# A sink-and-window attention ahead of two dense layers: attention stepped by whole blocks instead of half blocks, two head pairs to a score tile

## The chip, the cores and the metric

The kernel runs on one core of one Trainium2 chip. The metric is the device time of one execution in microseconds (us). PE is the matrix engine, DVE the vector engine, ACT the scalar engine, POOL the general engine; SP issues the loads and stores. PSUM is the memory that PE writes its results to: eight banks, each of 128 partitions by 512 floats.

## What is computed

An attention with sinks and a window (batch 2, 8 heads, 768 positions, 64 features; every query sees the first 4 keys and the last 128), then a layer whose activation is a rational function, then a layer with a squared ReLU:

```python
scores = scale * np.matmul(q, k.transpose(0, 1, 3, 2))
keep = is_sink | ((rel >= 0) & (rel < 128))            # is_sink: key < 4
scores = np.where(keep, scores, -1e9)
a = np.exp(scores - np.max(scores, axis=-1, keepdims=True))
a = a / (np.sum(a, axis=-1, keepdims=True) + 1e-09)
x = np.matmul(a, v)                                    # -> 1536 tokens x 512
h = x @ w_in                                           # 512 -> 2048
P = a0 + a1*h + a2*h*h + a3*h*h*h
Q = 1.0 + abs(b0)*abs(h) + abs(b1)*h*h
x = (P / (Q + 1e-6)) @ w_out                           # 2048 -> 512
h = np.maximum(x @ w_in2, 0.0)
out = (h * h) @ w_out2
```

## The kernel before, in words

**Blocks and half blocks.** The queries are cut into 12 blocks u of 128 (six for each batch). A block has four head pairs; a pair's two heads lie in partitions 0 to 63 and 64 to 127 of the keys and queries. The first block of a batch (u = 0 and 6) sees only its own keys; every other one sees the block before it too, and the sinks. The loop `for m in range(NM): step(m)` goes by half blocks: 24 steps m of two pairs, n = 2m and n + 1. Steps 24 and 25 finish the last block and run inside the first two slots of the layers that follow (`mid` of `slot`).

**What a step issues.** `scores(n)` puts a pair's scores into one of two tiles `ss` of PSUM (two banks each, one for each head) by four matmuls on 64x64 quarters of the array; DVE then folds the window's two triangles together (one copy_predicated, L368) and takes each head's masked row maximum (two reduces, L375). `expo(n)` lets ACT take the exponentials (L392, with row sums). `trans(m - 1)` transposes the half block before through the 128x128 array (L420); ACT copies the result to SBUF and POOL cuts it into two triangles `ph`. `pv(m - 2)` multiplies `ph` by the values (L453), into PSUM tile O. `sums(u)` adds eps to a block's row sums on ACT and takes reciprocals on DVE (L409); `sinks_t(u)` transposes the sink weights and reciprocals (L413); `sinks_and_sums(u)` adds the sinks' share to O (L465) and spreads the reciprocals to all rows of w (L469), with halves of the array, 64 rows by 128 columns; ACT copies w to `rb` (L471). `result(u)` is one DVE multiply of O by `rb` (L475), which ends the block and frees O. `parts_of(u)` splits it into two parts `xh` and `xl` for the layers (a cast on ACT, L482, a subtraction on POOL, L483).

**PSUM.** The score tiles take four banks, T (transposes, w, fill) two, U one, and O one: the sums of only one block can be open at a time.

**Ahead of and behind it.** Weights are loaded and split beside the attention (`w_step`: DVE L240, L246, L252; `w_fin`: ACT L273, POOL L274). At the start, PE runs matmuls of zeros on `wz` (`fill`, L496) while data come in, and masks are made on DVE, POOL and ACT (L102 to L147). In the layers, slot k issues `act_b(k - 1)` (ACT L637, L638, then DVE L641, L643, L645), `g1(k + 1)` (L591), `act_a(k)` (ACT L607 to L611), for slots 0 and 1 `cubic` (DVE L620) and a step of the attention, then `g2(k - 2)` (L670). What is issued to an engine runs on it in that order, and waits for what it needs.

Of the kernel before, what the change touches and what calls it, by code (L numbers as in the profile page):

```python
# [12 lines left out]
ALU = mybir.AluOpType  # L13
# [5 lines left out]
TWO32 = 4294967296.0  # L19
WS = 3  # L20
NW0 = 14
DENSE = {0: 5, 2: 4}
QP = 1.0 + 1e-6

LEAST = 2.0 ** -15 * 1.125
# [12 lines left out]
def kernel(  # L38
# [254 lines left out]
    def attention(ap, extra):  # L293
# [48 lines left out]
                keys[:, :, :, P:], keys[:, :, u % NB, 0:SK].unsqueeze(2).to_broadcast([P, NPR, NB, SK])  # L342
            )

        def scores(n):
            u, pr = divmod(n, NPR)
            i = u % NB
            t = ss[n % 2]
            d = [t[:, e] for e in range(2)]
            if i == 0:  # L350
                mask, co, bw = m_0, 0, P
                for e in range(2):
                    s = slice(D * e, D * e + D)
                    nc.tensor.matmul(
                        d[e][:, 0:P], lhsT=ld[u, "q"][s, pr, :], rhs=keys[s, pr, 0, 0:P], start=True, stop=True
                    )
            else:
                mask, co, bw = (m_1 if i == 1 else m_2), P, BS
                hf = P // 2
                for g in range(2):  # L360
                    for e in range(2):
                        s, r = slice(D * e, D * e + D), slice(hf * g, hf * g + BS + hf)
                        nc.tensor.matmul(  # L363
                            d[e][hf * g:hf * g + hf, r], lhsT=ld[u, "q"][s, pr, hf * g:hf * g + hf],
                            rhs=keys[s, pr, i - 1:i + 1, :].rearrange("p i n -> p (i n)")[:, r],
                            start=True, stop=True,
                        )
                nc.vector.copy_predicated(  # L368
                    out=t[:, :, BS:BS + P], mask=tri.unsqueeze(1).to_broadcast([P, 2, P]), data=t[:, :, 0:P]
                )  # L370
            ns = []
            for e in range(2):
                ix = u * H + 2 * pr + e
                t = ap.tile([P, 160], F32, name="ns", bufs=6)
                nc.vector.tensor_tensor_reduce(  # L375
                    out=t[:, 0:bw], in0=d[e][:, co:co + bw], in1=mask, scale=-scale, scalar=3.0e38,
                    op0=ALU.add, op1=ALU.min, accum_out=nmax[:, ix:ix + 1],
                )
                ns.append(t)
            kps[n] = ns  # L380

        def expo(n):
            u, pr = divmod(n, NPR)
            w = BS if u % NB else P
            if pr == 0:
# [19 lines left out]

        def sums(u):
            rs = rs_t.pop(u)
            nc.scalar.activation(out=rs, in_=rs, func=ACTF.Identity, bias=eps)
            nc.vector.reciprocal(out=sr[u % 2][:, HS:HS + H], in_=rs)  # L409

        def sinks_t(u):
            sd = ps_t(tail=u == NU - 1)
            nc.tensor.transpose(sd[:, 0:P], sr[u % 2], ident)  # L413
            sT[u] = ap.tile([P, P], F32, name="st", bufs=2)
            nc.scalar.copy(out=sT[u], in_=sd[:, 0:P])

        def trans(m):
            d = ps_t(tail=m == NM - 1)
# [4 lines left out]
            dv = d.rearrange("p (j t) -> p j t", j=4)  # L423
            h = [
                mp.tile([P, CT], F32R, tag=tag, name="ph", bufs=2).bitcast(F32).rearrange("p (j t) -> p j t", j=4)
                if m // 2 % NB or j else None for j, tag in enumerate(("gh", "gl"))
            ]
            if h[0] is None:
                nc.scalar.copy(out=h[1], in_=dv)
            else:  # L430
                c = ap.tile([P, 4, P], F32, name="pc", bufs=2)
                nc.scalar.copy(out=c, in_=dv)
                nc.gpsimd.affine_select(
                    out=h[0], in_=c, pattern=[[0, 4], [-1, P]], base=-1, channel_multiplier=1,
                    compare_op=ALU.is_ge, fill=0.0,
                )
                nc.gpsimd.affine_select(
                    out=h[1], in_=c, pattern=[[0, 4], [1, P]], base=0, channel_multiplier=-1,
                    compare_op=ALU.is_ge, fill=0.0,
                )  # L440
            pT[m] = h
# [16 lines left out]
                            )  # L458

        def sinks_and_sums(u):  # L460
            st, w = sT.pop(u), ps_t(tail=u == NU - 1)
            for r in range(NPR):
                cs = slice(r * P, (r + 1) * P)
                if u % NB:
                    nc.tensor.matmul(  # L465
                        ops[u][:, cs], lhsT=vs[u // NB][0:HS, cs], rhs=st[0:HS], start=False, stop=False,
                        skip_group_check=True,
                    )
                nc.tensor.matmul(w[:, cs], lhsT=heads[HS:, cs], rhs=st[HS:], start=True, stop=True)  # L469
# [41 lines left out]
        bd, moe, rest, heads = None, None, None, None  # L511
        sr = [ap.tile([P, P], F32, name=f"sr{j}") for j in range(2)]

        def step(m):
            w_fin()
            nonlocal bd, moe, rest, heads
            n, (u, a) = 2 * m, divmod(m, 2)
            if m < NM:
                scores(n)
            if a == 0 and u >= 1:  # L520
                sinks(u - 1)
                sums(u - 1)
            if m < NM:
                scores(n + 1)
                if n in DENSE:
                    fill(ps_t("T"), DENSE[n])
            if m == 0:
                rest = setup_rest(*next(masks), m_1, m_2, tri)
                next(rest)
                sink_keys(0)  # L530
            if a == 0 and 2 <= u <= NU:
                parts_of(u - 2)
            if m < NM:
                expo(n)
            if m in (1, 2):
                next(rest, None)
            if 0 < m <= NM:
                trans(m - 1)
            if m == 1:
# [5 lines left out]
            if a == 0 and u + 2 < NU:  # L545
                load(u + 2)
            if a == 0 and m < NM and u % NB == 0:
                load_sinks(u // NB)
            if m >= 5:
                next(moe, None)  # L550
                next(moe, None)
            if a == 1 and u >= 1:
                sinks_and_sums(u - 1)
            if 1 < m:
                pv(m - 2)
            if m < NM:
                expo(n + 1)
            if a == 0 and u >= 1:
                sinks_t(u - 1)
            if m == NM - 1:  # L560
                g1(0)
            if m < NM and a == 1 and u % NB == 0:
                if u:
                    sink_keys(u)
                sink_values(u // NB, bd)
            extra(m)
            if a == 1 and u >= 1:
                result(u - 1)

        for m in range(NM):  # L570
            step(m)
        for j in range(2):
            slot(j, lambda: step(NM + j))
        slot(2, after=lambda: parts_of(NU - 1))


# [447 lines left out]
    with tc.tile_pool(name="ap", bufs=1) as ap:  # L1024
        NM = NU * NPR // 2

        def extra(m):
            if m == 1:
                for _ in range(NWR):
                    w_load()  # L1030
            if m % 2:
                w_until(min(WS * NA, m - 1))
            if m == NM:
                conv["on"] = False
            if m == NM + 1:
                conv["tag"], conv["on"] = "O", True

        attention(ap, extra)
# [49 lines left out]
```

## Time and profile before

| | us |
|---|---|
| median of three runs (lowest, highest) | 617.02 (616.91, 618.19) |
| the profiled execution's own time | 617.14 |
| its span on the core | 615.4 |
| stretch from the first scores of block 0 to those of block 4 | 24.01 |
| stretch from there to the first matmul of the layers | 50.00 |
| stretch from there to the first matmul of `g2(0)` | 15.12 |

The profile is of one execution. Times of rows count from the span's start; the 1.74 us between span and time lie around the program. A row's busy time can overlap the next row's on the same engine, since instructions are pipelined: the distance between two starts is what an instruction costs its engine. PE is busy nearly all the time, so a shorter path on another engine is worth something only where PE waits for it, and less work on PE is worth something where nothing else becomes late.

### The profile page before, as it was taken

Reading aid. Unit: us, or ns where it says so; the run is one execution under the profiler, and the core shown is the slowest. Engines: PE = TensorE matmul, PEld = TensorE weight load, DVE = VectorE, ACT = ScalarE, POOL = GpSimd, SP = SyncE. Lnnn points to the kernel's source line nnn. Section 1 sums busy time; section 2 is a strip of 40 time slices with the busy share of each in tenths; the row PEclk is TensorE's granted clock in tenths of the full one; section 3 lists DMA queues with packets and bytes.
Section 4 is the critical chain, followed back from the end, with each engine's and each line's share of the span. In section 5 each row is a group of like instructions: output and inputs, shape, how many; then the busy total and the mean of one; then the engine's idle time right before and its main releaser. Section 6 shows DMA issues by size and latency. Waiting matters only on the chain.

```text
span 615.4 us, 9431 instructions
## 1 busy us (share of the span) xinstructions
PE 606.2 (99%) x3317; PEld 491.8 (80%) x3317; DVE 425.5 (69%) x863; ACT 355.4 (58%) x758; POOL 329.6 (54%) x293
## 2 busy tenths in 40 slices
PE   9999999999999999999999999999999999999995
PEld 6776788888888878888888888888888888888884
DVE  5888849998989989768768799598584432531411
ACT  5999978888886877877869443332331221222220
POOL 4676757677676766767759575354452212222211
PEclk9999999999999999999999999999999999999998
DMA  8866412332332332211111447467375345500102
GB/s 227 255 182 181 121 37 87 109 99 85 101 102 74 98 104 68 70 35 34 35 34 63 144 146 265 137 213 255 86 249 182 117 164 170 197 9 1 68 1 74
DMA packets 64231, 72.03 MB, mean 117 GB/s; under 512 B 15280, under 2 KB 55216, under 8 KB 64176
## 3 DMA queue, kind: packets, MB, share of 16 engines
q1 hardware_dynamic: 64032, 71.35, 37.9%
q8 instruction: 28, 0.46, 0.3%
q14 instruction: 27, 0.22, 0.1%
q10 hardware_dynamic: 144, 0.00, 0.0%
HBM read 68.20 MB, written 3.15 MB: 116 GB/s over the span
## 4 chain that ended last, share of the span: by engine, by line
PE 74%; DVE 13%; ACT 9%; issue 2%; DMA 1%; DVEq 0%; SPq 0%; ACTq 0%
PE s L670 32%; PE T L591 25%; PE U L591 7%; PE O L453 3%; DVE t L645 3%; DVE U L643 2%; PE s L363 2%; ACT U L637 2%; ACT U L638 2%; ACT gh L652 2%; ACT w L273 2%; PE T L420 2%; DVE t L641 1%; DVE O L240 1%; PE O L465 1%
## 5 line engine op out<-in xcount | busy, mean ns | idle before, releaser
L591 PE MATMUL T<-xh,w 128*128 128x512 f32 x640 | 210.6, 390 | 0.2 <-DVE t L620 0.2
L653 POOL TENSOR_TENSOR gl<-g,gh 128x512 fp32r<-128x512 f32 x48 | 62.2, 1296 | 157.8 <-ACT gh L652 157.8
L591 PEld LDWEIGHTS T<-xh,w 128*128 128x128 f32 x640 | 120.1, 188 | 26.3 <-DVE t L620 1.1
L670 PE MATMUL s<-gh,w 128*128 128x512 f32 x384 | 126.0, 389 | 0.0
L591 PE MATMUL T<-xl,w 128*128 128x512 f32 x320 | 124.5, 389 | 0.0
L670 PE MATMUL s<-w,gh 128*128 128x512 f32 x384 | 118.3, 389 | 0.0
L274 POOL TENSOR_TENSOR w<-wx,w 128x512 fp32r<-128x512 f32 x64 | 82.9, 1296 | 6.4 <-ACT w L273 6.4
L653 POOL TENSOR_TENSOR gl<-t,gh 128x512 fp32r<-128x512 f32 x48 | 62.3, 1299 | 44.5 <-ACT gh L652 42.8
L670 PEld LDWEIGHTS s<-gh,w 128*128 128x128 f32 x384 | 72.1, 188 | 15.0
L670 PEld LDWEIGHTS s<-w,gh 128*128 128x128 f32 x384 | 72.1, 188 | 14.9
L612 POOL TENSOR_TENSOR t<-t,ah 128x512 f32<-128x512 f32 x48 | 62.3, 1298 | 37.0 <-ACT t L609 35.1
L652 ACT CAST gh<-g 128x512 fp32r<-128x512 f32 x48 | 29.9, 623 | 82.1 <-PE s L670 74.8
L670 PE MATMUL s<-gl,w 128*128 128x512 f32 x192 | 74.7, 389 | 0.0
L670 PE MATMUL s<-w,gl 128*128 128x512 f32 x192 | 74.7, 389 | 0.0
L591 PEld LDWEIGHTS T<-xl,w 128*128 128x128 f32 x320 | 60.1, 188 | 12.3
L652 ACT CAST gh<-t 128x512 fp32r<-128x512 f32 x48 | 29.8, 622 | 45.6 <-DVE t L645 41.1
L641 DVE SCALAR_TENSOR_TENSOR t<-t,U 128x512 f32<-128x512 f32 x48 | 32.9, 686 | 28.1 <-ACT U L638 26.3
L626 DVE TENSOR_TENSOR g<-r,T 128x512 f32<-128x512 f32 x32 | 21.7, 682 | 42.2 <-ACT r L616 42.2
L616 ACT ACTIVATE r<-T 128x512 f32<-128x512 f32 x32 | 19.2, 600 | 53.2 <-PE T L591 53.1
L273 ACT CAST w<-wx 128x512 fp32r<-128x512 f32 x64 | 39.3, 616 | 6.4 <-DVE wx L252 6.4
L591 PE MATMUL U<-xh,w 128*128 128x512 f32 x128 | 42.1, 390 | 0.0
L670 PEld LDWEIGHTS s<-w,gl 128*128 128x128 f32 x192 | 36.0, 188 | 7.5
(136 smaller groups left out, 1022.4 us busy)
## 6 DMA issues: line engine op xcount, KB each, us to landing
wr<-in_w_in_dram SPq DMA_DIRECT2D x54, 512.0 KB, 3.7
wr<-in_w_out_dram SPq DMA_DIRECT2D x52, 512.0 KB, 3.7
qr<-in_q_dram SPq DMA_DIRECT2D x12, 256.0 KB, 4.0
keys<-in_k_dram SPq DMA_DIRECT2D x12, 256.0 KB, 4.5
vr<-in_v_dram SPq DMA_DIRECT2D x12, 256.0 KB, 5.0
wr<-in_v_dram SPq DMA_DIRECT2D x6, 512.0 KB, 4.8
out_dram<-part SPq DMA_DIRECT2D x12, 256.0 KB, 2.0
vsc<-in_v_dram SPq DMA_DIRECT2D x2, 16.0 KB
```

Of the source, the lines that this page charges most:

```text
L273: nc.scalar.copy(out=t[:, 0], in_=xf)
L274: nc.gpsimd.tensor_tensor(out=t[:, 1], in0=xf, in1=t[:, 0].bitcast(F32), op=ALU.subtract)
L453: nc.tensor.matmul(ops[u][D * e:D * e + D, pr * P:(pr + 1) * P], lhsT=ld[u - 1 + j, "v"][:, 2 * pr + e, :], rhs=pt[j][:, 2 * r + e], start ...
L591: nc.tensor.matmul(h, lhsT=wi[a][:, kk * P:(kk + 1) * P], rhs=(xh, xl)[b][c][:, kk, :], start=(kk == 0 and a + b == 0), stop=(kk == KD - 1 ...
L612: nc.gpsimd.tensor_tensor(out=t, in0=t, in1=ah, op=ALU.mult)
L616: nc.scalar.activation(out=r, in_=h, func=ACTF.Relu)
L626: nc.vector.tensor_tensor(out=g, in0=st.pop(k), in1=h, op=ALU.mult)
L641: nc.vector.scalar_tensor_tensor(out=t, in0=t, scalar=QP, in1=r0, op0=ALU.add, op1=ALU.mult)
L645: nc.vector.scalar_tensor_tensor(out=t3, in0=t3, scalar=fa[:, 0:1], in1=r0, op0=ALU.add, op1=ALU.mult)
L652: nc.scalar.copy(out=gh, in_=g)
L653: nc.gpsimd.tensor_tensor(out=gl, in0=g, in1=gh.bitcast(F32), op=ALU.subtract)
L670: nc.tensor.matmul(acc[L, g, c][m], lhsT=lh, rhs=rh, start=(f == f0 and a + b == 0), stop=(f == f1 and a == 1),)
```

## The change

`step(u)` goes by whole blocks, 14 calls in place of 26. Two pairs' scores share a tile, 248 columns apart, the second pair first; the four copies and eight maxima of a block are `fold(u, 0)` and `fold(u, 1)`, after the scores of both halves have been issued. The last stages come later: `sinks_t`, `pv` and `sinks_and_sums` of block u - 2 run in step u, `result` and `parts_of` of block u - 3, where `result(u - 1)` stood in step 2u + 1 before. `sinks_and_sums` works on 64x64 quarters, 16 matmuls where there were 8, directly ahead of the next block's scores, which are on quarters too. The eps add moves from ACT to DVE, the cast of `parts_of` from ACT to POOL. Three matmuls of zeros fewer stand in the first steps (6 for 5 + 4), the rest of the masks is made ahead of the first exponentials, loads are issued later by half a block or so, and T tiles give way to score tiles for the last two blocks.

Cut to its core:

```diff
-DENSE = {0: 5, 2: 4}
+DENSE = {0: (0, 6)}
+OFF = 248
-        def scores(n):
-            u, pr = divmod(n, NPR)
+        def scores(u, a):
             i = u % NB
-            t = ss[n % 2]
+            t = ss[a]
+            for k in (1, 0):
+                pr, o = 2 * a + k, OFF * k
+                d = [t[:, e, o:] for e in range(2)]
...
+        def fold(u, a):
+            pairs = [(k, ss[a][:, :, OFF * k:]) for k in (1, 0)]
+            for _, t in pairs:
+                if i:
+                    nc.vector.copy_predicated(
...
+            for k, t in pairs:
...
+                    nc.vector.tensor_tensor_reduce(
...
         def sums(u):
-            nc.scalar.activation(out=rs, in_=rs, func=ACTF.Identity, bias=eps)
+            nc.vector.tensor_tensor(out=rs, in0=rs, in1=eps.to_broadcast([P, H]), op=ALU.add)
...
         def sinks_and_sums(u):
...
+                for e in range(2):
+                    s = slice(r * P + D * e, r * P + D * e + D)
+                    x = slice(D * e, D * e + D)
+                    if u % NB:
+                        nc.tensor.matmul(
+                            ops[u][x, cs], lhsT=vs[u // NB][0:HS, s], rhs=st[0:HS], start=False, stop=False,
...
+                    nc.tensor.matmul(w[x, cs], lhsT=heads[HS:, s], rhs=st[HS:], start=True, stop=True)
...
         def parts_of(u):
-            nc.scalar.copy(out=h, in_=x)
+            nc.gpsimd.tensor_copy(out=h, in_=x)
...
-        def step(m):
+        def step(u):
...
+            if u < NU:
+                for a in range(2):
+                    scores(u, a)
+                    if u in DENSE:
+                        fill(ps_t("T"), DENSE[u][a])
...
+            if u < NU:
+                fold(u, 0)
+            if 0 <= u - 3:
+                result(u - 3)
+                parts_of(u - 3)
+            if u == 0:
+                sink_keys(0)
+                rest = setup_rest(*next(masks), m_1, m_2, tri)
+                next(rest)
+                next(rest)
+            if 0 <= u - 1 < NU:
                 sinks(u - 1)
                 sums(u - 1)
+            if 0 <= u - 2 < NU:
+                sinks_t(u - 2)
+            if u < NU:
+                expo(u * NPR + 1)
+            if 0 <= u - 1 < NU:
+                trans(2 * u - 2)
+                trans(2 * u - 1)
+            if u < NU:
+                expo(u * NPR)
+                fold(u, 1)
...
+            if 0 <= u - 2 < NU:
+                pv(2 * u - 4)
+                pv(2 * u - 3)
+            if 0 <= u - 1 < NU:
+                halves(2 * u - 2)
+                halves(2 * u - 1)
+            if u < NU:
+                expo(u * NPR + 3)
+            if 0 <= u - 2 < NU:
+                sinks_and_sums(u - 2)
+            if u < NU:
+                expo(u * NPR + 2)
```

On PE, a block in the middle of the attention (T, O and s are tiles of the PSUM areas named above, `pe` the exponentials, `sr` the sink weights and reciprocals) stood like this before:

```order
L363 MATMUL s<-keys,qr 64x200 x8
L420 MATMUL T<-ident,pe 128x128 x4
L453 MATMUL O<-ph,vr 64x128 x8
L413 MATMUL T<-ident,sr_154 128x128
L363 MATMUL s<-keys,qr 64x200 x8
L420 MATMUL T<-ident,pe 128x128 x4
L465 MATMUL O<-st,vm 128x128
L469 MATMUL T<-st,bd 128x128
```

Behind it came three more such pairs of L465 and L469 and eight L453. It stands like this now:

```order
L484 MATMUL T<-st,bd 64x128
L363 MATMUL s<-keys,qr 64x200 x16
L422 MATMUL T<-ident,sr_154 128x128
L429 MATMUL T<-ident,pe 128x128 x8
L465 MATMUL O<-ph,vr 64x128 x16
L480 MATMUL O<-st,vm 64x128
L484 MATMUL T<-st,bd 64x128
```

The kinds of matmul come in one run each instead of two, with 16 small ones (L480, L484 in turn) ahead of the next scores in place of eight between the halves.

On DVE, the same place before, with the multiply that ends a block (xf) ahead of the first pair's copy and maxima:

```order
L246 SCALAR_TENSOR_TENSOR U<-wr,U 128x512
L252 SCALAR_TENSOR_TENSOR wx<-wr,U 128x512
L475 TENSOR_TENSOR xf<-O,rb 128x512
L368 COPY_PREDICATED s<-tri,s 128x2x128
L375 ISA ns,nmax<-s,m_107 128x136
L375 ISA nmax 128x1
L375 ISA ns,nmax<-s,m_107 128x136
L375 ISA nmax 128x1
L409 RECIPROCAL sr_155<-rs 128x8
```

and now:

```order
L247 SCALAR_TENSOR_TENSOR U<-wr,U 128x512
L253 SCALAR_TENSOR_TENSOR wx<-wr,U 128x512
L375 COPY_PREDICATED s<-tri,s 128x2x128 x2
L384 ISA ns,nmax<-s,m_107 128x136
L384 ISA nmax 128x1
L384 ISA ns,nmax<-s,m_107 128x136
L384 ISA nmax 128x1
L384 ISA ns,nmax<-s,m_107 128x136
L384 ISA nmax 128x1
L384 ISA ns,nmax<-s,m_107 128x136
L384 ISA nmax 128x1
L490 TENSOR_TENSOR xf<-O,rb 128x512
```

The multiply (of the block three back) now comes behind a whole `fold`, that of the newest scores.

Where the attention ends and the layers begin, DVE had this before (t3, t and U belong to `act_b` and `cubic` of the layer; xf_1505 ends block 10, xf_1606 block 11):

```order
L475 TENSOR_TENSOR xf_1505<-O_1421,rb_1476 128x512
L620 SCALAR_TENSOR_TENSOR t3_1527<-t3_1527,fa_89,T_1488 128x512
L409 RECIPROCAL sr1_155<-rs_1407 128x8
L641 SCALAR_TENSOR_TENSOR t_1525<-t_1525,U_1560 128x512
L643 SCALAR_TENSOR_TENSOR U_1560<-t_1525,U_1560 128x512
L645 SCALAR_TENSOR_TENSOR t3_1527<-t3_1527,fa_89,U_1560 128x512
L620 SCALAR_TENSOR_TENSOR t3_1583<-t3_1583,fa_89,T_1510 128x512
L475 TENSOR_TENSOR xf_1606<-O_1547,rb_1596 128x512
```

and has this now (xf_1559 ends block 9, xf_1655 block 10, xf_1699 block 11):

```order
L649 SCALAR_TENSOR_TENSOR t3_1555<-t3_1555,fa_89,T_1518 128x512
L490 TENSOR_TENSOR xf_1559<-O_1470,rb_1514 128x512
L417 TENSOR_TENSOR rs_1441<-rs_1441,eps_90 128x8
L418 RECIPROCAL sr1_155<-rs_1441 128x8
L670 SCALAR_TENSOR_TENSOR t_1553<-t_1553,U_1628 128x512
L672 SCALAR_TENSOR_TENSOR U_1628<-t_1553,U_1628 128x512
L674 SCALAR_TENSOR_TENSOR t3_1555<-t3_1555,fa_89,U_1628 128x512
L649 SCALAR_TENSOR_TENSOR t3_1651<-t3_1651,fa_89,T_1538 128x512
L490 TENSOR_TENSOR xf_1655<-O_1584,rb_1626 128x512
L490 TENSOR_TENSOR xf_1699<-O_1663,rb_1697 128x512
```

The end of block 10 now stands behind the whole of `act_b(0)` and behind `cubic(1)`, where that of block 11 stood before; two blocks, not one, are still open when the layers begin.

## Rows read from the trace of the kernel before

**Rows 1.** Windows: span, busy us (instructions) of PE, PEld, DVE, ACT, POOL; clock, DMA

```profile
6.23:30.24 24.01, 23.76 (x272) 16.29 (x272) 19.27 (x94) 22.44 (x95) 15.21 (x24) 1.00 0.96 274
30.24:80.24 50.00, 49.93 (x675) 36.67 (x673) 42.34 (x187) 48.80 (x189) 34.59 (x44) 1.00 0.55 149
80.24:95.36 15.12, 15.12 (x104) 12.21 (x103) 6.95 (x11) 11.51 (x25) 8.19 (x9) 1.00 0.12 37
```

**Rows 2.** The page's slices: granted TensorE clock in tenths, 40 equal slices of the span

```profile
PEclk9999999999999999999999999999999999999998
```

**Rows 3.** Timeline of PE, block 4: start, busy us, engine, line, operation, tiles, shapes, count

```profile
30.24 0.91 PE L363 MATMUL s<-keys,qr 64*64 64x200 f32 x16
31.08 0.66 PE L420 MATMUL T<-ident,pe 128*128 128x128 f32 x4
31.67 1.09 PE L453 MATMUL O<-ph,vr 128*64 128x128 f32 x16
32.70 0.33 PE L413 MATMUL T<-ident,sr 128*128 128x128 f32 x1
32.95 0.91 PE L363 MATMUL s<-keys,qr 64*64 64x200 f32 x16
...
34.45 0.37 PE L465 MATMUL O<-st,vm 64*128 64x128 f32 x1
...
35.54 1.09 PE L453 MATMUL O<-ph,vr 128*64 128x128 f32 x16
```

**Rows 4.** Timeline of PE, block 7, whose first half needs half the value matmuls

```profile
50.61 0.66 PE L453 MATMUL O<-ph,vr 128*64 128x128 f32 x8
51.19 0.33 PE L413 MATMUL T<-ident,sr 128*128 128x128 f32 x1
```

**Rows 5.** Timeline of DVE, block 4; in brackets idle time before and what ended it

```profile
30.46 0.69 DVE L475 TENSOR_TENSOR xf<-O,rb 128x512 f32<-128x512 f32 x1 [0.36 <-PE O L453]
31.07 0.42 DVE L368 COPY_PREDICATED s<-tri,s 128x256 f32<-128x256 int32 x1
...
31.96 0.20 DVE L409 RECIPROCAL sr<-rs 128x8 f32<-128x8 f32 x1
...
33.59 0.43 DVE L368 COPY_PREDICATED s<-tri,s 128x256 f32<-128x256 int32 x1 [0.54 <-PE s L363]
...
34.50 0.42 DVE L368 COPY_PREDICATED s<-tri,s 128x256 f32<-128x256 int32 x1
...
35.51 0.69 DVE L240 TENSOR_SCALAR U<-wr 128x512 int32<-128x512 int32 x1
```

**Rows 6.** Timelines of ACT and of POOL at the start

```profile
7.13 0.40 ACT L392 ACTIVATE pe<-ns,nmax 128x128 f32<-128x128 f32 x1 [5.04 <-DVE nmax L375]
...
7.53 0.39 ACT L392 ACTIVATE pe<-ns,nmax 128x128 f32<-128x128 f32 x1
...
8.08 0.50 POOL L142 TENSOR_TENSOR su<-su 128x128 f32<-128x128 f32 x1 [6.22 <-DVE su L124]
```

**Rows 7.** Timeline of PE where the attention ends

```profile
87.46 0.48 PE L591 MATMUL T<-xh,w 128*128 128x512 f32 x1
...
90.38 0.37 PE L465 MATMUL O<-st,vm 64*128 64x128 f32 x1
```

**Rows 8.** Timelines of ACT and DVE at the same place

```profile
87.90 0.70 ACT L637 ACTIVATE U<-t,qb 128x512 f32<-128x512 f32 x1
88.63 0.58 ACT L638 ACTIVATE U<-U 128x512 f32<-128x512 f32 x1
...
91.59 0.59 ACT L471 COPY rb<-s 128x512 f32<-128x512 f32 x1 [0.45 <-PE s L469]
...
89.32 0.69 DVE L641 SCALAR_TENSOR_TENSOR t<-t,U 128x512 f32<-128x512 f32 x1 [3.12 <-ACT U L638]
...
91.44 0.74 DVE L620 SCALAR_TENSOR_TENSOR t<-t,fa,T 128x512 f32<-128x512 f32 x1
```

**Rows 9.** The page's groups: line, engine, operation, tiles, count; busy us, mean ns; idle before

```profile
L274 POOL TENSOR_TENSOR w<-wx,w 128x512 fp32r<-128x512 f32 x64 | 82.9, 1296 | 6.4 <-ACT w L273 6.4
```

More of the change, by code (lines that the diff above doesn't have):

```diff
@@ new lines, in scores @@
+            t = ss[a]
+            for k in (1, 0):
+                pr, o = 2 * a + k, OFF * k
+                d = [t[:, e, o:] for e in range(2)]
+                if i == 0:
+                    for e in range(2):
+                        s = slice(D * e, D * e + D)
+                        nc.tensor.matmul(
+                            d[e][:, 0:P], lhsT=ld[u, "q"][s, pr, :], rhs=keys[s, pr, 0, 0:P], start=True, stop=True
+                        )
+                else:
+                    hf = P // 2
+                    for g in range(2):
+                        for e in range(2):
+                            s, r = slice(D * e, D * e + D), slice(hf * g, hf * g + BS + hf)
+                            nc.tensor.matmul(
+                                d[e][hf * g:hf * g + hf, r], lhsT=ld[u, "q"][s, pr, hf * g:hf * g + hf],
+                                rhs=keys[s, pr, i - 1:i + 1, :].rearrange("p i n -> p (i n)")[:, r],
+                                start=True, stop=True,
+                            )
@@ new lines, in fold @@
+        def fold(u, a):
+            i = u % NB
+            mask, co, bw = (m_0, 0, P) if i == 0 else (m_1 if i == 1 else m_2, P, BS)
+            pairs = [(k, ss[a][:, :, OFF * k:]) for k in (1, 0)]
+            for _, t in pairs:
+                if i:
+                    nc.vector.copy_predicated(
+                        out=t[:, :, BS:BS + P], mask=tri.unsqueeze(1).to_broadcast([P, 2, P]), data=t[:, :, 0:P]
+                    )
+            for k, t in pairs:
+                n = u * NPR + 2 * a + k
+                ns = []
+                for e in range(2):
+                    ix = 2 * n + e
+                    x = ap.tile([P, 160], F32, name="ns", bufs=6)
+                    nc.vector.tensor_tensor_reduce(
+                        out=x[:, 0:bw], in0=t[:, e, co:co + bw], in1=mask, scale=-scale, scalar=3.0e38,
+                        op0=ALU.add, op1=ALU.min, accum_out=nmax[:, ix:ix + 1],
+                    )
+                    ns.append(x)
+                kps[n] = ns
@@ L384, in expo @@
             w = BS if u % NB else P
-            if pr == 0:
+            if u not in pe_t:
                 pe_t[u] = ap.tile([P, NPR, 2, ROW], F32, name="pe", bufs=2)
@@ L417, in trans @@
         def trans(m):
-            d = ps_t(tail=m == NM - 1)
+            d = ps_t(tail=m >= NM - 2)
             for j in range(4):
@@ L422, in trans, with halves @@
                 )
-            dv = d.rearrange("p (j t) -> p j t", j=4)
+            c = ap.tile([P, 4, P], F32, name="pc", bufs=2)
+            nc.scalar.copy(out=c, in_=d.rearrange("p (j t) -> p j t", j=4))
+            pT[m] = c
+        def halves(m):
+            c = pT[m]
             h = [
@@ L428, in trans @@
             if h[0] is None:
-                nc.scalar.copy(out=h[1], in_=dv)
+                nc.gpsimd.tensor_copy(h[1], c)
             else:
-                c = ap.tile([P, 4, P], F32, name="pc", bufs=2)
-                nc.scalar.copy(out=c, in_=dv)
                 nc.gpsimd.affine_select(
@@ L460, in sinks_and_sums @@
         def sinks_and_sums(u):
-            st, w = sT.pop(u), ps_t(tail=u == NU - 1)
+            st, w = sT.pop(u), ps_t(tail=u >= NU - 2)
             for r in range(NPR):
                 cs = slice(r * P, (r + 1) * P)
[L464 to L469, printed above, removed]
+                for e in range(2):
+                    s = slice(r * P + D * e, r * P + D * e + D)
+                    x = slice(D * e, D * e + D)
+                    if u % NB:
+                        nc.tensor.matmul(
+                            ops[u][x, cs], lhsT=vs[u // NB][0:HS, s], rhs=st[0:HS], start=False, stop=False,
+                            skip_group_check=True,
+                        )
+                    nc.tensor.matmul(w[x, cs], lhsT=heads[HS:, s], rhs=st[HS:], start=True, stop=True)
             rb[u] = ap.tile([P, CT], F32, name="rb", bufs=1)
@@ L544, in step @@
                 moe = setup_moe()
-            if a == 0 and u + 2 < NU:
-                load(u + 2)
-            if a == 0 and m < NM and u % NB == 0:
-                load_sinks(u // NB)
[L549 to L560, printed above, removed]
+            if u + 2 < NU:
+                load(u + 2, "qk")
+            if 1 <= u < NU - 1:
+                load(u + 1, "v")
+            if u < NU and u % NB == 0:
+                load_sinks(u // NB)
+            if u >= 3:
+                for _ in range(4):
+                    next(moe, None)
+            if u == NU - 1:
                 g1(0)
-            if m < NM and a == 1 and u % NB == 0:
-                if u:
-                    sink_keys(u)
+            if u < NU and u % NB == 1:
                 sink_values(u // NB, bd)
[L566 to L571, printed above, removed]
+            extra(u)
+            if u == NU + 1:
+                result(NU - 1)
+        for u in range(NU):
+            step(u)
         for j in range(2):
-            slot(j, lambda: step(NM + j))
+            slot(j, lambda: step(NU + j))
         slot(2, after=lambda: parts_of(NU - 1))
@@ L1025, with extra @@
         NM = NU * NPR // 2
[L1027 to L1033, printed above, removed]
+        def extra(u):
+            for _ in range((1, 1, 2)[u] if u < 3 else 0):
+                w_load()
+            w_until(min(WS * NA, 2 * u))
+            if u == NU:
                 conv["on"] = False
-            if m == NM + 1:
+            if u == NU + 1:
                 conv["tag"], conv["on"] = "O", True
```

58 lines of the change are left out of this document (6 added, 52 removed).

## The prediction, made before the result was known

> **What bounds the kernel now.** I read the windows first: in the attention's middle PE is busy 49.93 of 50.00 us, over eight blocks, so 6.25 a block, at full clock [rows 1, 2]. ACT is close behind with 48.80; DVE has 42.34, POOL 34.59. In the first stretch ACT, with 22.44 of 24.01, is the tighter one beside PE. Then the timeline of PE, for what its work consists of [rows 3, 4], and that of DVE for who waits for whom [rows 5]. PE waits for almost nothing, so the change can gain only by shortening PE's own work, and loses wherever PE gets a wait. The order rows say where to look for waits: every `pv(2u - 4)` writes the one O tile, so it waits for `result(u - 3)`, which now stands on DVE behind `fold(u, 0)`, which waits for PE's scores of the same step. That is a loop through two engines and back inside each block.
>
> **PE's own work gets shorter.** From starts in [rows 3]: scores 31.08 - 30.24 = 0.84, transposes 0.59, `pv` 32.70 - 31.67 = 1.03, `sinks_t` 0.25, sinks and sums 35.54 - 34.45 = 1.09. A block had 2 x (0.84 + 0.59 + 1.03) + 0.25 + 1.09 = 6.26, the 6.25 of the window. Eight `pv` records take 51.19 - 50.61 = 0.58 [rows 4], sixteen 1.03, so eight more of a kind cost 0.45, 0.056 each, and 1.03 - 16 x 0.056 leaves some 0.14 for starting such a run. In the same way four transposes take 0.59 and one 0.25, 0.11 each, with 0.14 to 0.15 over. I take 0.15 a run; before had eight runs a block (two of each kind, one `sinks_t` inside the transposes' kind but in a run of its own, one of sums), the change has three (quarters; transposes; `pv`). Five saved are 0.75 to 0.8. The sixteen quarter matmuls are four at a time where there were eight halves two at a time: as many columns one behind the other, so 1.09 - 0.15, about 0.92. PE alone would need 1.53 (scores) + 1.2 and 0.1 (transposes) + 1.89 (`pv`) + 0.92, about 5.4 in all with the hand-overs between, for 6.25. If no wait came, 0.8 x 11 blocks = 9 us would be won: this is the case for the change.
>
> That a change of tile mode drains the engine is also what the Trainium skill says (TensorEngine Tiling (Array Packing), Key Properties); it gives no price, and the 0.15 is the trace's.
>
> **The loop that takes it back.** Its links, from the start of a block's scores: (1) To DVE's first copy 33.59 - 32.95 = 0.64 for one pair [rows 3, 5]; the semaphore now comes behind both pairs of the tile, 0.34 more (half of 0.69), less about 0.05 for the saved start: 0.92. (2) `fold`: one pair takes 31.96 - 31.07 = 0.89, two 1.78; a copy followed by a wait for a second engine made that 35.51 - 34.50 = 1.01 [rows 5], so 0.11 more: 1.89. (3) `result` 0.69. (4) From DVE's end to PE's start, no row alone, since PE's waits are hidden; bounded by nothing and by what link 1 has over half the scores' time, 0.64 - 0.35 = 0.29; 0.15, the middle, taken. (5) `pv`, both halves, 1.89. (6) sinks and sums 0.92, and the next scores follow at once. Sum 6.46 a block. PE has only 1.53 + 1.3 of work to put between (1) and (4), which take 3.65, so it idles about 0.8. The saved 0.8 becomes a wait.
>
> Independent groups of matmuls should rotate through PSUM banks, so that emptying one overlaps the next, says the Trainium skill (Perfetto Trace Analysis, Optimizing Tensor Performance, Matmuls). By that rule one O bank costs time as soon as its emptying is late; the order rows put it late.
>
> DVE alone has 42.34 / 8 = 5.3 busy a block, plus the eps add (0.2 by the nearest row, the reciprocal) and gaps between its records, about 6.05: it stays under the loop, but not by much. ACT sheds the cast (about 0.5) and the eps add (0.2) of its 6.1. POOL takes the cast: no row shows it; a copy is bounded by nothing (hidden) and by the 1.30 of its subtraction of the same shape [rows 9], 34.59 / 8 + 1.30 = 5.6 a block, still under 6.46; I cost it at nothing, hidden by the loop, and 0.1 to 0.2 a block if POOL is late for `pv`.
>
> **Start.** ACT's first exponential comes now behind the rest of the masks: DVE's window work follows `fold(0, 0)`, POOL's first instruction on it starts about where it did, 8.08, two of them and three of ACT's make 9.6, for 7.13 [rows 6]. From there ACT has up to the end of block 2's exponentials 24 x 0.40 = 9.5 [rows 6], copies of transposes and the like 3.4 (four of some 0.5 and the last mask, a `rb` and two small ones), and 0.7 idle as before (24.01 - 22.44, less the 0.9 ahead of the first): 23.2. Then PE's transposes 1.2, hand-over 0.2, `pv` 1.89, sums 0.92: the scores of block 4 start at 27.4, for 30.24: -2.8. But by then one block less has been finished, since the pipeline is a block deeper; this is repaid at the end.
>
> **Middle.** Blocks 4, 5, 7, 9, 10, 11: 6 x 6.46 = 38.8. Block 6 has no copies (0.9 less in the fold): 5.5, about what PE and ACT need anyway. In block 8 the first batch-block's `pv` is half as long, loop 5.6, so DVE's 6.05 counts. Sum 50.3 for 50.00: the layers start at 77.75, 2.5 earlier than 80.24.
>
> **End.** Up to `g2(0)` there were 15.12 [rows 1]. Two open blocks now: one more `sinks_t` (0.1 to 0.26), transposes 0.6, `pv` 1.9, sums 0.92: 3.4. And a wait: the `pv` of block 11 needs `result(10)`. This needs `rb(10)` on ACT, 0.2 + 0.48 behind the sums' end; but DVE does first `act_b(0)` and `cubic(1)`, and ACT's part of `act_b(0)` stands behind `rb(10)`. From the sums' end: 0.67 to the end of `rb`; 0.73 + 0.58 + 0.11 to DVE's L641 (87.90, 88.63, 89.32 [rows 8]); 91.44 - 89.32 = 2.12 to `cubic`; 0.67 and 0.62 for this and `result`; 0.15: 5.65. PE has meanwhile `g1(2)`, 90.38 - 87.46 = 2.92 [rows 7], and a transpose of 0.26. It waits some 2.4. So 3.4 + 2.4 = +5.8.
>
> **Sum.** -2.5 + 5.8 = +3.3 against the profiled run's 617.14: 620.4. The median is 0.12 lower than that run, which I leave as noise. Behind `g2(0)` the order of the layers is the old one; weights were ahead there, so I cost it at nothing; if weights are late, some tenths.
>
> **Rivals.** (a) The loop is looser than I made it (a lower link 1 or 2, or other hand-overs): then DVE's 6.05 sets the pace, the layers start 6 x 0.41 = 2.5 earlier, 617.9. It speaks for it that the links come from one pair and were put together; against it, that each has its row. (b) The same, and the wait at the end is covered, because DVE's rows of `act_b(0)` come early: 615.5. Against it: the order of ACT. (c) Neither binds, and PE works at 5.5 a block in the middle, end as in (a): 6 x 0.96 + 0.5 = 6.3 less than my forecast, 614.1; with the end covered 611.7. This is the change working as built; it would need `result` to be done before `fold`'s wait, which the order excludes unless the scores' semaphore comes much earlier. (d) The slower side of mine: TensorE's clock is not at 2.4 GHz throughout. Before, it was granted in full in every slice but the last [rows 2], while PE idled 0.07 in 50.00 and 0.25 in 24.01 [rows 1]; now PE idles 0.8 a block and some microseconds at the start. If matmuls take twice as long at the lower level of 1.2 GHz, which no row here shows, 6 us of PE's work at the start at that level, half of it on the path, give +3, 623.4. My forecast itself lies on the slower side; the sign turns where the loop is under about 6.05 a block (a).
>
> **How the numbers follow.** Within 0.2% (1.2 us) is about what a measurement of this kernel can tell from no change. Forecast 0.58; (d), or a loop of 6.7, 0.12; (a) 0.12; (b) 0.06; (c) 0.12. The forecast's own range is 618.3 to 622.5 (links 4 and 2 by 0.2 a block, six blocks, and the wait at the end by 0.8). Slower takes the forecast, (d) and a sixth of (a): 0.72; same, the rest of (a) and half of (b): 0.13; faster, (c) and the rest of (b): 0.15. The range that holds 8 in 10 goes from 616.2 to 623.4.
>
> **What the profile after would show.** Right: PE idle 0.7 to 0.9 in each middle block, ended by DVE's `result`; scores to scores 6.4 to 6.6; the multiply directly behind the second pair's last maximum, and `pv` starting 0.1 to 0.3 behind it; a PE gap of 2 to 3 us ahead of the last `pv`, and `cubic` and `result` just ahead of its end; scores of block 4 near 27.4, and the layers' first matmul near 77.8. Wrong: PE without gaps in the middle (c), DVE without gaps at 6.05 a block (a), granted clock under 1.00 in a slice (d), or POOL's triangles (`ph`) as releaser of `pv`.

## The result, and the profile after

The changed kernel takes 624.64 us (median of 4, 624.03 to 625.23) for 617.41 (616.91 to 618.19) of the kernel before on the same chips: a ratio of 1.0116, interval 1.0098 to 1.0133. It is slower by some 7 us, where 3.3 were forecast. The profiled execution took 624.49 with a span of 622.7.

Where the 7.3 us of span came from is seen when both timelines of PE are cut at the same four places: the first scores of block 0, those of block 4, the first matmul of the layers (`g1(0)`), the first of `g2(0)`, and the last matmul of all.

| stretch, us | before | after | difference | forecast |
|---|---|---|---|---|
| start: block 0's scores to block 4's | 24.01 | 21.03 | -2.98 | -2.8 |
| middle: to `g1(0)` | 50.00 | 51.18 | +1.18 | +0.3 |
| end: to `g2(0)` | 15.12 | 22.79 | +7.67 | +5.8 |
| layers: to the last matmul's start | 512.25 | 513.61 | +1.36 | 0 |

The windows of the changed kernel (span; busy us and instructions of PE, PEld, DVE, ACT, POOL; clock; DMA), to be held against [rows 1]:

```profile
6.40:27.44 21.04, 16.65 (x241) 12.40 (x244) 18.00 (x95) 17.70 (x77) 13.09 (x22) 1.00 1.03 293
27.44:78.62 51.18, 44.27 (x800) 36.48 (x793) 45.32 (x196) 44.66 (x178) 40.57 (x54) 1.00 0.56 153
78.62:101.41 22.79, 20.25 (x190) 16.88 (x187) 6.68 (x12) 11.92 (x25) 12.58 (x15) 0.93 0.08 24
```

PE's work in the middle did shrink, from 49.93 to 44.27. PE now stands idle for 6.9 us there (51.18 less 44.27), and the middle is longer all the same. At the end the granted clock is below 1.00 where it was not before. The page's slices show it in the seventh, for [rows 2]:

```profile
PEclk9999998999999999999999999999999999999999
```

**The middle.** PE's timeline of the changed kernel, blocks 4, 5 and 6 (in brackets idle time and what ended it), for [rows 3]:

```profile
27.44 1.53 PE L363 MATMUL s<-keys,qr 64*64 64x200 f32 x32
...
30.77 0.66 PE L429 MATMUL T<-ident,pe 128*128 128x128 f32 x4 [1.10 <-ACT st L424]
31.36 1.97 PE L465 MATMUL O<-ph,vr 128*64 128x128 f32 x32
...
34.18 1.53 PE L363 MATMUL s<-keys,qr 64*64 64x200 f32 x32
...
37.86 1.97 PE L465 MATMUL O<-ph,vr 128*64 128x128 f32 x32 [0.86 <-DVE rs L417]
...
43.17 0.66 PE L429 MATMUL T<-ident,pe 128*128 128x128 f32 x4 [0.52 <-ACT st L424]
```

and DVE's, for [rows 5], with the eps add of block 4 in the first line and block 5's chain below it:

```profile
30.89 0.90 DVE L417 TENSOR_TENSOR rs<-rs,eps 128x8 f32<-128x8 f32 x1
...
35.11 0.89 DVE L375 COPY_PREDICATED s<-tri,s 128x256 f32<-128x256 int32 x2
...
37.02 0.69 DVE L490 TENSOR_TENSOR xf<-O,rb 128x512 f32<-128x512 f32 x1
37.63 0.15 DVE L417 TENSOR_TENSOR rs<-rs,eps 128x8 f32<-128x8 f32 x1
```

In block 5 the loop of the prediction can be read link by link: scores at 34.18, DVE's copies at 35.11 (0.93), the multiply at 37.02 (fold 1.91), its end at 37.71 (0.69), `pv` at 37.86 (0.15). The profile names L417, the add right behind the multiply, as releaser; it starts before the multiply's end, so the name is that of the last event before the start. In blocks 4 and 6 another wait came first: the second half's transposes wait for ACT's copy `st` (L424), since `sinks_t` and the transposes share the two T tiles.

**The end.** PE, DVE and ACT of the changed kernel where the attention ends, for [rows 7, 8]:

```profile
85.42 1.97 PE L465 MATMUL O<-ph,vr 128*64 128x128 f32 x32
...
91.21 0.27 PE L422 MATMUL s<-ident,sr 128*128 128x128 f32 x1
94.03 3.57 PE L465 MATMUL O<-ph,vr 128*64 128x128 f32 x32 [2.54 <-DVE xf L490]
```

```profile
90.42 0.69 DVE L670 SCALAR_TENSOR_TENSOR t<-t,U 128x512 f32<-128x512 f32 x1 [5.02 <-ACT U L667]
91.14 0.69 DVE L672 SCALAR_TENSOR_TENSOR U<-t,U 128x512 f32<-128x512 f32 x1
91.88 0.75 DVE L674 SCALAR_TENSOR_TENSOR t<-t,fa,U 128x512 f32<-128x512 f32 x1
92.54 0.74 DVE L649 SCALAR_TENSOR_TENSOR t<-t,fa,T 128x512 f32<-128x512 f32 x1
93.20 0.68 DVE L490 TENSOR_TENSOR xf<-O,rb 128x512 f32<-128x512 f32 x1
...
88.52 0.59 ACT L486 COPY rb<-s 128x512 f32<-128x512 f32 x1 [2.35 <-PE s L484]
89.00 0.70 ACT L666 ACTIVATE U<-t,qb 128x512 f32<-128x512 f32 x1
```

`rb` of block 10 is there at 89.11. DVE takes the multiply that needs it at 93.20, behind four others. PE waits 2.54 us and then takes 3.57 us for the same 32 records that took 1.97 at 85.42. The window of those records shows the clock:

```profile
91.50:94.00 2.50, 0.00 (x0) 0.00 (x1) 2.35 (x4) 0.90 (x3) 1.33 (x2) 0.99 0.00 0
94.03:97.53 3.50, 3.50 (x32) 3.28 (x33) 0.00 (x0) 0.00 (x0) 1.79 (x2) 0.52 0.00 0
```

A granted 0.52 of full speed is nearly all at the lower level of 1.2 GHz, directly behind 2.5 us in which PE did nothing. The next section tests whether that is the cause.

**The layers.** In the 30 us behind `g2(0)` PE waited for nothing before; in the changed kernel it waits once there, for the cubic on DVE:

```profile
121.44 0.50 PE L620 MATMUL T<-xh,w 128*128 128x512 f32 x1 [0.50 <-DVE t L649]
```

This and smaller delays around it make 1.36 us up to the end. Some 100 us later each kernel shows one more wait for DVE, 0.16 us before and 0.17 now.

### The profile page after: what moved, and what is told of

It reads as the page before. It is cut to its first block, busy times and chain, and to the rows that moved or that the text cites. A ratio compares the mean times of both kernels' runs of the same rounds, so it can differ in the third digit from the quotient of the medians.

```text
span 622.7 us, 9780 instructions
## 1 busy us (share of the span) xinstructions
PE 599.8 (96%) x3490; PEld 492.4 (79%) x3490; DVE 428.5 (69%) x875; ACT 347.6 (56%) x734; POOL 338.6 (54%) x309
## 4 chain that ended last, share of the span: by engine, by line
PE 81%; DVE 10%; ACT 6%; issue 1%; POOL 0%; DVEq 0%; ACTq 0%
PE s L699 37%; PE T L620 30%; PE U L620 7%; PE O L465 3%; ACT pe L401 2%; PE O L480 1%; DVE ns L384 1%; DVE t L674 1%; DVE U L672 1%; DVE t L670 1%; DVE wx L253 1%; PE s L511 1%; DVE xf L490 1%; ACT U L666 1%; DVE part L728 1%
## 5 line engine op out<-in xcount | busy, mean ns | idle before, releaser
L655 DVE TENSOR_TENSOR g<-r,T 128x512 f32<-128x512 f32 x32 | 21.8, 683 | 42.5 <-ACT r L645 42.5
L699 PEld LDWEIGHTS s<-gl,w 128*128 128x128 f32 x192 | 36.0, 188 | 7.6
```

The costliest lines, as they stand in the source:

```text
L655: nc.vector.tensor_tensor(out=g, in0=st.pop(k), in1=h, op=ALU.mult)
L699: nc.tensor.matmul(acc[L, g, c][m], lhsT=lh, rhs=rh, start=(f == f0 and a + b == 0), stop=(f == f1 and a == 1),)
```

## The experiments

Two theories stood against each other for the middle: the loop through the one O tile, and the plain amount of work on DVE, ACT and POOL. For the end the question was whether the wait alone cost, or also the clock behind it; for the layers, whether their loss came from the end.

### The multiply ahead of the fold

```diff
+            if 0 <= u - 3:
+                result(u - 3)
             if u < NU:
                 fold(u, 0)
             if 0 <= u - 3:
-                result(u - 3)
                 parts_of(u - 3)
```

> The changed kernel with one line moved: result(u-3) ahead of fold(u,0) on DVE. Loop theory (PE's value matmuls wait for the one O bank, which is freed behind a whole fold): the loop is gone, the middle stretch (scores of block 4 to the layers) falls from 51.2 us to 46 to 48, what DVE's own work of 5.7 to 6.0 a block allows, and the time from 624.6 to 620 to 622. Rival (DVE or ACT sets the pace by its amount of work, not by the order): within 1 us of 624.6. Start and end as in the changed kernel in both.

Measured: 620.47 us (620.3 to 620.55), 1.0048 of before, interval 1.0031 to 1.0065. The middle took 48.19 us, 3.0 less than in the changed kernel, and the start 20.43 for 21.03; the end, 22.84, was that of the changed kernel. So the order of one instruction on DVE cost 3 us in the middle, as the loop theory wants it, though the middle stayed just above the 46 to 48 that were expected. PE still idles 4.0 us of it, for 6.9 in the changed kernel, mostly for ACT's copy `st` (the middle's window; then PE, block 9):

```profile
26.94:75.13 48.19, 44.15 (x800) 36.13 (x793) 45.71 (x193) 43.04 (x177) 41.02 (x55) 1.00 0.63 167
...
59.72 0.65 PE L429 MATMUL T<-ident,pe 128*128 128x128 f32 x4 [0.91 <-ACT st L424]
```

A variant had the multiply inside the fold, between copies and maxima:

```diff
-        def fold(u, a):
+        def fold(u, a, between=None):
...
+            if between:
+                between()
             for k, t in pairs:
                 n = u * NPR + 2 * a + k
...
-                fold(u, 0)
+                fold(u, 0, (lambda: result(u - 3)) if u >= 3 else None)
...
```

> The changed kernel with result(u-3) inside fold(u,0), between the copies and the maxima. Loop theory: like result_first or up to 0.7 us better, since DVE's copies no longer wait behind a result that waits for ACT's rb; 619.5 to 621.5. Rival (amount of work): within 1 us of 624.6.

Measured: 621.0 us (620.03 to 622.44). The middle of the profiled execution took 49.29, at clock 1.00; its granted clock in the start was 0.92 (6 to 20 us). It says no more than that this place is no better than the one ahead of the fold, and that the 0.7 us more that were thought possible did not come.

### The end: the wait, and the clock behind it

The multiply of block 10 ahead of `act_b(0)`, by a call at the top of slot 1 (its old call in the step is taken out):

```diff
...
+            if ahead:
+                ahead()
             if 0 <= k - 1 < K:
                 act_b(k - 1, lambda: w_until(min(due(k), wst["int"] + 1)))
...
-            slot(j, lambda: step(NU + j))
+            slot(j, lambda: step(NU + j), ahead=(lambda: result(NU - 2)) if j else None)
```

> The changed kernel with result(10) ahead of act_b(0) on DVE. Theory of the end (the last value matmuls wait 2.5 us for result(10), behind act_b(0) and cubic(1), and then run at half clock because PE stood still): wait and half clock both go, -2.6 - 1.6 = -4.2, to 620.4. Rival 1 (half clock for another reason): the wait alone goes, 622.0. Rival 2 (the engines behind are late anyway, the layers take back what the wait gives): 623 to 624.6, with more PE idle in the layers between 104 and 122 us.

Measured: 620.36 us (619.51 to 620.88). The end took 18.58 instead of 22.79, -4.2, as the first theory had it. The multiply runs at 89.66 and `pv` follows the transpose without a wait, at full clock (PE; then the window from `g1(0)` to `g2(0)`):

```profile
91.69 0.27 PE L422 MATMUL s<-ident,sr 128*128 128x128 f32 x1
91.89 1.97 PE L465 MATMUL O<-ph,vr 128*64 128x128 f32 x32
...
79.10:97.67 18.57, 18.57 (x190) 15.30 (x187) 6.78 (x12) 11.92 (x25) 12.57 (x15) 1.00 0.10 30
```

To part the wait from the clock, ten matmuls of zeros were put into the wait, and nothing else moved:

```diff
+            if u == NU + 1:
+                fill(ps_s()[:, 0], 10)
             if 0 <= u - 2 < NU:
                 pv(2 * u - 4)
```

> The changed kernel with ten matmuls of zeros (about 2.3 us) on PE in the wait ahead of the last value matmuls; nothing else is moved. If the half clock came from PE standing still: the value matmuls take 1.9 instead of 3.5 us at clock 1.00, 623.0, the wait for result(10) itself unchanged. If it did not: 624.6, clock still 0.83 in that stretch. If the 1.3 us that the layers lost come from DVE and ACT being behind PE there, they grow by up to the 1.6 won, and the time stays at 624 to 624.6.

Measured: 622.65 us (622.36 to 623.13). `pv` starts 2.82 us behind the transpose ahead of the wait, as in the changed kernel (2.82), but takes 1.97:

```profile
90.92 2.54 PE L511 MATMUL s<-wz 128*128 128x512 f32 x10
93.71 1.97 PE L465 MATMUL O<-ph,vr 128*64 128x128 f32 x32 [0.25 <-DVE xf L490]
```

The end took 21.22, 1.57 less. So of the 4.2 us some 2.6 were the wait and 1.6 the clock. All four times lie below all four of the changed kernel, and with PE kept at work the clock stayed up. The layers did not take the 1.6 back: their stretch stayed at 513.52.

PE's standing still is not the whole cause, though. Seven profiles of this series have this wait of 2.5 us unfilled, and six of them show the lower clock behind it. The seventh, first_eps (below), does not (PE):

```profile
91.67 1.97 PE L465 MATMUL O<-ph,vr 128*64 128x128 f32 x32 [2.54 <-DVE xf L490]
```

Its end took 21.17, as with the fill. So the wait can bring the clock down and does not always; what else decides is not shown.

### The layers' loss

tail_result still lost 1.0 us in the layers (513.28 for 512.25). The next run had, besides, block 11's sinks and sums between the two halves of its `pv`, as the kernel before:

```diff
                 pv(2 * u - 4)
+                if u == NU + 1:
+                    sinks_and_sums(u - 2)
                 pv(2 * u - 3)
...
```

> tail_result, and for block 11 the sinks and sums moved between the two halves of its value matmuls, as the kernel before has them; so ACT gets block 11's reciprocals about 0.9 us earlier beside PE. Theory of the layers' loss (1.3 us in the changed kernel, 1.0 in tail_result: DVE and ACT enter the layers later beside PE than before, because the sums now end behind all value matmuls): the loss between g2(0) and the last matmul falls from 1.0 to 0.3 or less, 619.6 to 619.9 against 620.4, the stretch g1(0) to g2(0) grows by 0.1 to 0.2 for another change of mode. Rival (weights are split later because the loads are): no change, 620.4 to 620.6.

Measured: 619.71 us (618.5 to 619.8). The layers took 512.28, the value of before: the loss is gone, and the end is 0.15 longer, as expected for a change of mode. The two later kernels with this edit have 512.31 and 512.30, those without it 513.20 to 513.61. The reading is that it matters where DVE stands beside PE when the layers begin. DVE starts `act_b(1)` at 94.01 before, 1.35 us ahead of `g2(0)`; at 101.12 in the changed kernel, 0.29 ahead; here at 96.87, 1.31 ahead, since ACT gets to copy block 11's reciprocals earlier (DVE before, changed and here):

```profile
94.01 0.69 DVE L641 SCALAR_TENSOR_TENSOR t<-t,U 128x512 f32<-128x512 f32 x1
...
101.12 0.69 DVE L670 SCALAR_TENSOR_TENSOR t<-t,U 128x512 f32<-128x512 f32 x1 [0.31 <-ACT U L667]
...
96.87 0.68 DVE L673 SCALAR_TENSOR_TENSOR t<-t,U 128x512 f32<-128x512 f32 x1
```

For the next 20 us DVE has almost no gap (20.3 of 21.8 us busy in the changed kernel), so what it lacks at the start PE later waits for. The total fell by 0.65, not by 1.0: in the profiled executions the start took 22.21 us for tail_result's 21.00, at a lower clock behind a wait of 1.18 us, and block 0's scores came 0.8 us earlier.

### Quarters or halves

> The changed kernel with sinks and sums in 64 by 128 halves, eight matmuls as before, at their new place ahead of the scores. If the quarters save just a change of tile mode (0.11 to 0.15 a block, eleven blocks, all of it in the loop): 1.2 to 1.6 more, 625.9 to 626.3. Rival (quarters run four at a time and cost no more than halves, but the mode change is hidden beside the wait): within 0.4 of 624.6.

The edit takes the loop over `e` out of `sinks_and_sums`:

```diff
-                for e in range(2):
...
+                nc.tensor.matmul(w[:, cs], lhsT=heads[HS:, cs], rhs=st[HS:], start=True, stop=True)
```

Measured: 625.11 us (624.11 to 626.59). The middle took 52.22, 1.04 longer over its eight blocks:

```profile
28.78:81.00 52.22, 45.43 (x674) 37.21 (x672) 45.20 (x196) 45.10 (x178) 40.37 (x54) 1.00 0.55 148
```

That is 0.13 a block, and by luck inside the 0.11 to 0.15 of the first theory, whose sum had counted three blocks of the start too: blocks 7 and 10, where the loop alone counts, lost 0.23 and 0.22, block 4 lost 0.04, and block 5, whose next scores are on halves anyway, nothing. The executions scatter over 2.5 us, and the profiled one lost clock in the start (0.94 in the first 20 us), so the time alone would not tell; the middle, at clock 1.00 in both, does. In such a block the quarters are worth somewhat more than one change of mode.

### The start: masks behind the exponentials, and the clock again

```diff
                 next(rest)
-                next(rest)
...
                 expo(u * NPR + 2)
             if u == 0:
+                next(rest)
```

> The changed kernel with the second mask's ACT part behind block 0's exponentials, as before. If the first exponential (9.6 in the changed kernel) sets the start: it goes to about 7.2 to 7.5, and the scores of block 4 come 1 to 2 us earlier, 622.6 to 623.6. Rival (DVE's folds or PE's waits for them set the start): exponentials earlier, scores of block 4 within 0.4 of 21.0 us behind those of block 0, 624.6.

Measured: 623.98 us (623.72 to 624.15). The first exponential came at 7.30 for 9.73, but the start took 20.91 for 21.03, and the windows of 13 to 19 us show a lower clock, behind a wait of 1.65 us on PE:

```profile
13.00:16.00 3.00, 1.35 (x21) 0.74 (x16) 2.87 (x12) 3.00 (x14) 2.39 (x3) 0.84 1.11 314
16.00:19.00 3.00, 3.00 (x25) 2.44 (x23) 2.67 (x15) 2.28 (x10) 0.06 (x1) 0.60 1.05 321
```

It looked as if the clock had eaten the gain. Nine more matmuls of zeros should have given it back (`DENSE = {0: (0, 6), 1: (3, 0), 2: (6, 0)}`):

> masks, with three matmuls of zeros between the two halves of block 1's scores and six between those of block 2, where PE waited 0.8 and 1.7 us for DVE in masks and then ran at clock 0.6 to 0.84. If PE's standing still lowers the clock at the start and this took what the earlier exponentials gave: clock 1.00 up to block 4, whose scores come 19.4 to 20.0 us behind block 0's (masks 20.9), and about 1 us less in all, 623. Rival (ACT's and DVE's work sets the start at full clock as well): 20.7 to 21.0, 624.

Measured: 624.5 us (624.39 to 624.74). The clock was 1.00 in both windows, and the start still took 20.78. This guess was wrong: in this kernel the start got only 0.13 us shorter with the clock back. ACT and DVE, busy for 17.9 and 18.0 of the 20.8 us, are the likely limit; no run parts them. It is not so everywhere: in tail_split the lower clock fell 3 us later, and the start was 1.2 us longer.

### What is left when the loop is gone

In result_first DVE had one gap in the middle (0.96 us, block 7), with the eps add at 0.36 to 0.99 us in seven of eight blocks, and PE waited for `st`. Either could set the pace. The eps add alone back on ACT:

```diff
-            nc.vector.tensor_tensor(out=rs, in0=rs, in1=eps.to_broadcast([P, H]), op=ALU.add)
+            nc.scalar.activation(out=rs, in_=rs, func=ACTF.Identity, bias=eps)
```

> result_first with the eps add back on ACT, ACT's order unchanged. In result_first the add took 0.4 to 0.99 us on DVE where it met an instruction of POOL, for 0.16 alone, and DVE had no gaps. If DVE's amount sets the pace there: 0.4 a block less, middle 45.5 to 46 instead of 48.2, 618. If ACT's order (st behind eight other things, PE waiting for it) sets it too: the eps add lengthens that path by 0.2, middle 48 to 49, 620.5 to 621.5; then the 1.0 us of best_try's middle came from the order on ACT.

Measured: 621.28 us (620.3 to 622.58), middle 48.67: not better than 48.19, rather worse. DVE's amount of work alone did not set the pace; PE's waits still end with ACT's copy (1.14 us in block 9). That copy stood behind `rb`, two exponentials, a weight cast, the copy `sr` and now the eps add.

Now all together: result_first, tail_result, tail_split, the eps add on ACT, and `sinks_t` with its copy ahead of `sinks`, `sums` and the weight cast:

```diff
-            w_fin()
...
+            if 0 <= u - 2 < NU:
+                sinks_t(u - 2)
             if 0 <= u - 1 < NU:
                 sinks(u - 1)
                 sums(u - 1)
-            if 0 <= u - 2 < NU:
-                sinks_t(u - 2)
+            w_fin()
```

> result_first, tail_result and tail_split together, with the eps add back on ACT (off DVE, which in result_first had no gaps at 6.08 a block) and ACT's st copy ahead of its sr copy and weight cast (PE waited 0.4 to 0.9 a block for st in result_first). If DVE's amount and that ACT order are what is left: middle 45.5 to 47 us (before 50.0, changed 51.2), end 18.6, layers' loss under 0.3: 614 to 616 in all, faster than the kernel before by 1.5 to 3. Rival (something else sets 6.0 a block, POOL above all): middle 48, 617 to 618, no difference from before.

Measured: 614.47 us (614.25 to 615.09), 0.9951 of before, interval 0.9935 to 0.9968: faster than both kernels. Middle 47.19, end 18.71, layers 512.31. The middle is 1.0 better than in result_first. The eps add alone had gained nothing, so the order on ACT is in it; whether that order would do without the eps add off DVE was not parted. The middle stayed just above the 45.5 to 47 that were expected. With masks and the fill on top:

> best_try with masks and the same fill. If both helped alone they help here: scores of block 4 come 19 to 19.5 us behind block 0's (best_try 20.3), 613 to 613.8. Rival: 614.5 as best_try.

Measured: 613.73 us (613.38 to 614.34), 0.9941 of before, interval 0.9925 to 0.9958, the lowest median of all, though its interval overlaps that of best_try. Its windows, stretch by stretch:

```profile
6.37:25.71 19.34, 18.56 (x250) 13.89 (x253) 16.74 (x91) 17.50 (x76) 12.69 (x21) 1.00 1.02 287
25.71:72.89 47.18, 44.11 (x801) 36.31 (x793) 42.91 (x193) 44.62 (x189) 41.21 (x55) 1.00 0.66 179
72.89:91.61 18.72, 18.72 (x190) 15.28 (x187) 8.17 (x13) 13.76 (x33) 12.47 (x15) 1.00 0.10 31
```

Here masks and fill together are worth 0.9 us in the start (19.34 for 20.27), where they gave 0.25 to the changed kernel. That ACT's new order lets them through is a guess; no run parts the two. PE still idles 3.1 us in the middle; what sets its 5.9 us a block was not tried further.

## Why the prediction was too low

**What held.** The sign, and the loop with its links: 0.93, 1.91, 0.69, 0.15 for the forecast 0.92, 1.89, 0.69, 0.15. Blocks 7 and 10 took 6.49 and 6.50 for 6.46, blocks 8 and 9 together 12.45 for 12.51. PE's own work fell about as computed: 5.66 us less in the middle, 0.7 a block for 0.75 to 0.8; that is 5.53 a block, where the forecast's terms, said to make about 5.4, add up to 5.64. The scores of block 4 started at 27.44 for 27.4, in part by luck: the forecast hung the start on ACT's first exponential, and in masks that came 2.4 us earlier and moved the start by 0.12. Multiply to multiply, block 8 took 5.94 with DVE free of gaps, for the 6.05 that was put down to DVE. result_first shows that the loop made some 3 us of the saved work a wait; when it was gone, the wait for `st` took part of its place.

**Middle, +0.9 over the forecast.** The step that failed: the loop was taken for the only wait. In block 4 (6.74) and block 6 (5.79 for 5.5) the second transposes waited 1.10 and 0.52 for ACT's `st`, whose place on ACT the prediction did not look at, although `sinks_t` had been moved ahead of the transposes and takes one of the two T tiles from them. In block 6 `st` stands on ACT behind seven instructions since the scores began, in block 4 behind twelve: five small ones that prepare the layers' constants (28.96 to 29.81) are among them, once only. Blocks 5 and 11 had 0.11 for a change of mode, as quarters are followed there by other than quarters. The eps add, costed at 0.2, took 0.90 and 1.08 us in blocks 4 and 6, but no wait of PE is seen to come of it.

**End, +1.9 over the forecast.** The wait was sized at 2.4 and measured 2.54. The step that failed is the next one: the value matmuls behind it were put in at their full-clock 1.89, and took 3.50 from start to start, nearly all at half the clock. The rival on the clock, (d), had the right mechanism in the wrong place: it looked for the idle PE at the start and in the blocks, not where the forecast itself had put the longest wait. tail_fill showed 1.57 us for it, and first_eps that such a wait does not always cost it. The rows of before could not have told which it would be.

**Layers, +1.4 where nothing was forecast.** The step that failed is this one: "the order of the layers is the old one; weights were ahead there, so I cost it at nothing". The order was the old one, but DVE and ACT entered it 1.06 us later beside PE, and DVE was nearly full there. tail_split showed it by putting the sums back. Half of this step could have been read from the order rows: block 11's sums now stand behind all of its `pv`.

The three, 0.9, 1.9 and 1.4, are the 4.1 us between the forecast of 620.4 and the profiled 624.49, but for rounding.

## What to carry to other kernels

When matmuls are packed tighter, look for every tile with one buffer (or two) that PE writes, and find where on the freeing engine's queue the freeing instruction now stands; a loop through two engines can take the saved work back, and moving one instruction ahead gave 3 us here. A pipeline made one stage deeper is paid for at its end: what was hidden by full blocks there stands behind whatever the next phase has queued. Where a forecast has PE standing still for microseconds, price what follows it at the lower clock as a case of its own (here 1.6 us, in six of seven profiles), and where a phase begins with an engine nearly full, carry its delay on.

## What the runs showed of the hardware

A wait of 2.54 us on PE was followed by 3.50 us of matmuls at a granted clock of 0.52, and the same wait filled with matmuls of zeros by none. The wait alone does not decide: in first_eps the same 2.54 us, unfilled, left the clock at 1.00, and in the start a wait of 1.18 us was followed by the lower clock in tail_split and not in the changed kernel. Waits of 0.2 to 1.1 us in the blocks of the middle left the clock at 1.00.

The eps add, an operation of 128 by 8 on DVE from SBUF to SBUF, took 0.15 to 0.16 us in six of the eight middle blocks and 0.90 and 1.08 in the others. In these its end falls on the end of an instruction of POOL that had begun before it. In block 4 of the changed kernel (POOL's weight subtraction ends at 31.76, the add at 31.79):

```profile
30.49 1.27 POOL L275 TENSOR_TENSOR w<-wx,w 128x512 fp32r<-128x512 f32 x1 [1.63 <-ACT w L274]
31.71 0.62 POOL L497 CAST xh<-xf 128x512 fp32r<-128x512 f32 x1
```

DVE's other instructions on either side show no such stretching. Most of them read or write PSUM; but the reciprocal behind the add, from SBUF to SBUF with one tensor read where the add reads two, took 0.20 throughout, beside POOL's casts too (at 37.82, beside the cast from 37.77 to 38.38). That the two engines share something that such an add needs is a reading, not shown by a run of its own.
